# Moving one load and one conversion in a queue of weight preparations, and its last pieces to a later stage

## Chip, core and metric

One core of one Trainium2 chip runs the whole program in one launch. The metric is the device time of an execution in microseconds (us), the median of several runs. Lower is better.

## The reference

Chunked attention with a little memory, then two multilayer perceptrons (MLPs) on its 3072 rows of 512 values. Both MLPs go 512 to 2048 to 512. All weights arrive as float64.

```python
a = softmax(scale * q_c @ k_full.T)      # 32 rows, 64 or fewer keys
x = a @ v_full                           # -> 3072 x 512
h = x @ moe_w_in;   g = h - np.tanh(h);  x = g @ moe_w_out
h = x @ moe2_w_in
g = np.where(h >= 1, h, np.where(h <= -1, 0.0, (h + 1)**2 / 4))
return g @ moe2_w_out
```

## The kernel before

Products keep nearly full float32 precision by splitting each operand into a rounded high part and the remainder, `hi` and `lo`, and adding three matmuls (hi with hi, hi with lo, lo with hi).

**Steps.** MLP 1 and most of the attention run in 96 steps, 6 blocks of 512 rows by 16 slices of the hidden width. In the loop over `i`, step `i` does this in the program's order: ScalarE (ACT) rounds slice `i+2` of the input weights to its high part (`whi`, line 172), VectorE (DVE) subtracts to get the low part (`wlo`, line 179); ACT and DVE split an older gated slice (`ghi` line 214, `glo` line 215); SyncE (SP) issues DMAs; TensorE (PE) does the 12 matmuls of `hidden(i+1)` (line 559); ACT takes its tanh (line 572) and DVE subtracts it (line 573); then the events named `behind` run, and PE does the 12 matmuls of `output(i-16)` (line 597). The tanh of step `i` writes the buffer that the `glo` of the same step still reads, so ACT's tanh comes after DVE's `glo`. Each engine works its instructions off in program order, and SP does so with its DMAs, waits included. From step 30 on, every fourth step also has a group of attention; its exponentials (line 428) are on ACT, its transposes (lines 446 and 480) on PE. The last 2 blocks of MLP 1's output product, and all of MLP 2, use a scheme of seven products (Strassen's) that needs prepared weights.

**The three stages after that.** In stage G the output product of the last two blocks is made in 7 passes of 8 products, `("G", -1, k)`, k from 0 to 55 (`last_product`, line 886; six matmuls each). Then MLP 2 runs in three parts of products named `("P", sb, q, i)` and `("G", sb, k)`.

**The queue.** Weight preparation for MLP 2 is cut into pieces in the list `todo`. Each step calls `work(c)` last among its `behind` events: `c` is added to a credit, and pieces are taken, their cost deducted, as long as the credit is above 0. There are 16 slice pairs, n = 0 to 15; "n.0" and "n.1" below are the two slices of pair n. For a slice,

- `load` is one 512 KB DMA from SP (line 125) into `stage0` or `stage1`. It must wait until the buffer's last reader is done;
- `act` is two instructions on ACT (lines 137 and 140);
- `mag` is two on DVE (lines 146, 147) and `sign` two more on DVE (lines 155, 160), the last readers of the stage buffer.

A pair then has sums of quarters on DVE (line 210), rounded high parts on ACT (`prep_hi`, line 237), low parts on DVE (`prep_lo`, line 243), and stores from SP (`prep_store`, lines 314, 316). The pieces of the special weights for stage G (`own`) are put at the head of the queue at steps 48, 52, 56, 60, 66, 70, 74 and 78. In stage G and in MLP 2, `work` is called after each product.

Of the kernel before, what the change touches and what calls it, by code (L numbers as in the profile page):

```python
# [77 lines left out]
def tile_memory_attention_two_mlps(  # L78
# [40 lines left out]
    def load_weights(phase, which, fc, tag=None):  # L119
        src = ((w1_in, w1_out), (w2_in, w2_out))[phase][which]  # L120
        if tag is None:
            tag = f"stage{loaded[0] % STAGES}"
            loaded[0] += 1
        stage = wide.tile([128, 512, 2], I32, tag=tag, name=f"stage{phase}{which}_{fc}")
        nc.sync.dma_start(out=stage, in_=src[fc])
        stage_t[phase, which, fc] = stage
# [3 lines left out]
    def round_act(phase, which, fc, part=None, tag=None):  # L130
        stage = stage_t[phase, which, fc]
        low, high = stage[:, :, 0], stage[:, :, 1]
        if part != 1:
            t = slot(tag or (f"raw1_{fc % 3}" if which else f"raw0_{fc}"), f"raw{phase}{which}_{fc}")
            raw_t[phase, which, fc] = t

            nc.scalar.activation(out=t, in_=high.bitcast(F32), func=AF.Abs)
        if part != 0:

            nc.scalar.activation(out=low, in_=low.bitcast(U32), func=AF.Copy, scale=2.0 ** -29)  # L140

    def round_mag(phase, which, fc):
        t = raw_t[phase, which, fc]
        mag = t.bitcast(I32)

        nc.vector.tensor_scalar(out=t, in0=t, scalar1=F64_LOW, scalar2=F64_HIGH, op0=ALU.max, op1=ALU.min)
        nc.vector.tensor_scalar(
            out=mag, in0=mag, scalar1=3, scalar2=0x3FFFFFF8,
            op0=ALU.logical_shift_left, op1=ALU.bitwise_and,
        )  # L150

    def round_sign(phase, which, fc):
        stage = stage_t.pop((phase, which, fc))
        bits = raw_t[phase, which, fc].bitcast(I32)
        nc.vector.scalar_tensor_tensor(
            out=bits, in0=stage[:, :, 1], scalar=-0x40000000, in1=bits, op0=ALU.bitwise_and, op1=ALU.bitwise_or
        )

        eng = nc.vector if phase else nc.gpsimd
        eng.tensor_tensor(out=bits, in0=bits, in1=stage[:, :, 0], op=ALU.add)  # L160
# [92 lines left out]
    def prep_items():  # L253
        def load(n, i):
            if n < len(PAIRS):
                w, q = PAIRS[n]
                load_weights(1, w, q + i * HALF, f"stage{i}")

        def act(n, i):
            w, q = PAIRS[n]  # L260
            round_act(1, w, q + i * HALF, tag=f"prep{i}")

        def mag(n, i):
            round_mag(1, PAIRS[n][0], PAIRS[n][1] + i * HALF)

        def sign(n, i):
            round_sign(1, PAIRS[n][0], PAIRS[n][1] + i * HALF)

        load(0, 0)
        load(0, 1)  # L270
        late = [[], []]
        for n, p in enumerate(PAIRS):
            todo.extend([
                (0.0, [(act, n, 0)] + late[0]),
                (0.9, [(act, n, 1), (mag, n, 0)] + late[1]),
                (1.2, [(sign, n, 0)]),
                (0.9, [(load, n + 1, 0), (mag, n, 1)]),
                (1.2, [(sign, n, 1)]),
                (1.4, [(prep_hi, *p, 0), (prep_sums, *p)]),
                (0.6, [(load, n + 1, 1), (prep_hi, *p, 3), (prep_lo, *p, 0)]),  # L280
                (0.4, [(prep_hi, *p, 1), (prep_lo, *p, 3)]),
                (0.6, [(prep_store, *p, 0), (prep_hi, *p, 2), (prep_lo, *p, 1)]),
                (0.6, [(prep_store, *p, 3), (prep_lo, *p, 2)]),
            ])
            late = [[(prep_store, *p, 1)], [(prep_store, *p, 2)]]
        todo.extend((0.6, x) for x in late)
# [11 lines left out]
    def work(c):  # L298
        if not todo:
            return  # L300
        credit[0] += c
        while todo and credit[0] > 0:
            cost, calls = todo.pop(0)
            credit[0] -= cost
            for f, *args in calls:
                f(*args)
        if not todo:
            spare.extend(f"prep{i}" for i in range(9))
# [560 lines left out]
    def last_product(e):  # L869
        _, sb, k = e  # L870
        i, q = PASSES[k // HALF], k % HALF
        a = i in (1, 6, 7, 4)
        if q == 0 and i in (1, 2, 5):
            bank[a] = [ps_g[0].tile([128, 512], F32, tag=f"g{c}{1 - a}", name=f"acc{i}_{sb}_{c}") for c in range(2)]
        rests()
        prepare(sb, k)
        hi_g, lo_g = gsplit.pop((sb, k))
        tag, t = w_t.pop(e)
        hi, lo = t[:, :256], t[:, 256:]
        first, last = i in (1, 2, 5) and q == 0, q == HALF - 1  # L880
        products = [(j, c) for j in range(3) for c in range(2)]
        if last:
            products.sort(key=lambda p: p[1])
        for j, c in products:
            w, g = ((hi, hi_g), (lo, hi_g), (hi, lo_g))[j]
            nc.tensor.matmul(  # L886
                bank[a][c], w[:, c * 128:(c + 1) * 128], g,
                start=first and j == 0, stop=last and j == 2, skip_group_check=True,
            )
        load_w(tag)  # L890
        flush()
        if k in SUMS_AT[sb < 0]:
            g_sums(sb, *SUMS_AT[sb < 0][k])
        for j in range(1, GSETS):
            prepare(sb, k + j)
        if last:
            done(sb, i, bank[a])
        nxt = sb + 1
        if nxt < NSB:
            for f, *args in x_at[sb < 0].get(k, ()):  # L900
                f(nxt, *args)
# [66 lines left out]
    for w in range(2):  # L968
        for fc in range(FC):
            p = fc - EARLY + w * (FC + 2)  # L970
# [6 lines left out]
    for q, o in OWN_AT.items():  # L977
        at_step(rounds, o, own, q, o - FC)
    at_step(behind, PREP_FROM - 3, prep_items)
    for i in range(PREP_FROM, NS):  # L980
        at_step(behind, i + 0.9, work, (CREDIT if i < PLAIN + 12 else (3.2,) * 4 if i < LAST else (0.85,) * 4)[i % 4])
# [110 lines left out]
    for e in plan:  # L1092
        if e[0] == "P":
            product(e)
        else:
            last_product(e)
        if e[0] == "G" and e[1:] == (-1, NG2 - 1):
            spare.extend(f"y{i}" for i in range(KC))
        if e[0] == "G" and e[1] < 0:
            work(0.5 if 12 <= e[2] < 20 else 0.25 if e[2] >= 29 else 0.0)  # L1100
        elif e[0] == "P":
            work(0.1)
    assert not todo
# [49 lines left out]
```

## Time and profile before

| | |
|---|---|
| median of 3 runs | 1108.26 us (1106.98 to 1109.68) |
| profiled execution, its own time | 1105.85 us |
| span of its trace, first to last instruction | 1104.1 us |
| granted TensorE clock, mean | 0.994 |
| busy: PE, weight load, DVE, ACT, GpSimd | 96%, 78%, 76%, 61%, 4% |
| DMA traffic | 259.37 MB, 235 GB/s on average |

Steps 30 to 79 lie at about 190 to 520 us of the span, steps 80 to 95 at 520 to 563 us, stage G at 564 to 640 us, MLP 2 behind that. The span is 1.75 us shorter than the execution's own time. The mean clock is a share of TensorE's full 2.4 GHz; its other level, 1.2 GHz, shows as 0.5.

### The profile page before, as it was taken

The numbers are of one execution on the slowest core, as the hardware profiler recorded it, in microseconds if no ns is written. First come the engines' busy times: TensorE is split into PE (matmuls) and PEld (weight loads), VectorE is DVE, ScalarE is ACT, GpSimd is POOL, SyncE is SP. The second block draws the span as 40 slices with busy tenths as digits, with TensorE's granted clock in tenths as the row PEclk, the third lists the DMA queues.
The fourth block names the chain that finished last, engine by engine and source line by source line (L and its number), as shares of the span: only waits on it lengthen the run. The fifth ranks groups of instructions, "written<-read, shape, count | busy, mean of one in ns | idle before, by whom it ended". The sixth has DMA issues, their size and how long they took to land.

```text
span 1104.1 us, 21244 instructions
## 1 busy us (share of the span) xinstructions
PE 1065.4 (96%) x7607; PEld 861.9 (78%) x7607; DVE 842.2 (76%) x1490; ACT 669.1 (61%) x1353; POOL 42.5 (4%) x38
## 2 busy tenths in 40 slices
PE   7899999999999997999999999999999999999998
PEld 3677888877787776887787888887888888888887
DVE  5699977787787886888999946688557697467854
ACT  3566766656565554565565757767377766477553
POOL 1132221000000000000000000000000000000000
PEclk9999999999999999999999999999999999999999
DMA  9997887799899898768749786677776787766674
GB/s 219 251 258 209 265 232 223 218 294 304 234 295 297 266 289 269 221 213 262 230 136 332 246 270 193 194 250 222 240 205 193 205 278 213 231 195 194 200 206 148
DMA packets 211945, 259.37 MB, mean 235 GB/s; under 512 B 65408, under 2 KB 128896, under 8 KB 211840
## 3 DMA queue, kind: packets, MB, share of 16 engines
q1 hardware_dynamic: 211840, 258.01, 78.1%
q8 instruction: 61, 1.00, 0.4%
q14 instruction: 44, 0.36, 0.1%
HBM read 199.23 MB, written 58.72 MB: 234 GB/s over the span
## 4 chain that ended last, share of the span: by engine, by line
PE 73%; DVE 10%; ACT 6%; DMA 6%; SPq 2%; issue 2%; ACTq 0%; DVEq 0%
PE acc L886 19%; PE h L559 16%; PE qa L798 12%; PE acc L597 7%; PE qc L798 6%; PE qb L798 3%; DMA stage<-w_in 2%; PE acc_-1_0_7237 L886 2%; PE acc_-1_1_7238 L886 2%; DVE glo L215 2%; ACT e L428 1%; ACT g L572 1%; DVE wlo L179 1%; DVE prepl L243 1%; PE a L460 1%
## 5 line engine op out<-in xcount | busy, mean ns | idle before, releaser
L886 PE MATMUL acc<-ghi,inG 128*128 128x512 f32 x672 | 183.2, 390 | 0.0
L572 ACT ACTIVATE g<-h 128x512 f32<-128x512 f32 x96 | 57.5, 599 | 162.8 <-DVE glo L215 97.1
L886 PEld LDWEIGHTS acc<-ghi,inG 128*128 128x128 f32 x672 | 126.2, 188 | 26.1
L215 DVE TENSOR_TENSOR glo<-g,ghi 128x512 fp32r<-128x512 f32 x174 | 117.9, 686 | 31.8 <-ACT ghi L214 31.1
L798 PE MATMUL qa<-xc,inP 128*128 128x512 f32 x576 | 139.3, 389 | 0.0
L214 ACT ACTIVATE ghi<-g 128x512 fp32r<-128x512 f32 x174 | 108.2, 631 | 46.5 <-PE acc L886 24.5
L798 PEld LDWEIGHTS qa<-xc,inP 128*128 128x128 f32 x576 | 108.2, 188 | 22.4
L559 PE MATMUL h<-xh,whi 128*128 128x512 f32 (+2 forms) x392 | 108.3, 399 | 12.0 <-ACT whi L172 8.9
L559 PE MATMUL h<-xl,whi 128*128 128x512 f32 (+2 forms) x392 | 106.7, 395 | 1.4 <-issue 1.3
L886 PE MATMUL acc<-glo,inG 128*128 128x512 f32 x336 | 107.4, 391 | 0.3 <-DVE glo L215 0.2
L559 PE MATMUL h<-xh,wlo 128*128 128x512 f32 (+2 forms) x392 | 105.7, 392 | 0.3
L179 DVE TENSOR_TENSOR wlo<-raw,whi 128x512 fp32r<-128x512 f32 x112 | 80.6, 720 | 26.8 <-ACT whi L172 26.8
L573 DVE TENSOR_TENSOR g<-h,g 128x512 f32<-128x512 f32 x96 | 66.0, 688 | 40.8 <-ACT g L572 40.5
L559 PEld LDWEIGHTS h<-xh,whi 128*128 128x128 f32 x392 | 72.2, 191 | 30.0 <-ACT whi L172 11.0
L736 ACT ACTIVATE t<-g,half 128x512 f32<-128x512 f32 x72 | 52.2, 725 | 62.2 <-DVE g L732 62.2
L559 PEld LDWEIGHTS h<-xl,whi 128*128 128x128 f32 x392 | 74.5, 192 | 18.3 <-issue 1.6
L559 PEld LDWEIGHTS h<-xh,wlo 128*128 128x128 f32 x392 | 73.9, 191 | 17.1 <-DVE wlo L179 2.0
L597 PE MATMUL acc<-ghi,whi 128*128 128x512 f32 x256 | 74.6, 406 | 1.4 <-ACT y L606 1.4
L172 ACT ACTIVATE whi<-raw 128x512 fp32r<-128x512 f32 x112 | 71.0, 634 | 7.5 <-POOL raw L160 7.4
L886 PEld LDWEIGHTS acc<-glo,inG 128*128 128x128 f32 x336 | 63.0, 188 | 14.7 <-DVE glo L215 1.8
L798 PE MATMUL qc<-xc,inP 128*128 128x512 f32 x288 | 73.1, 389 | 0.0
L597 PE MATMUL acc<-ghi,wlo 128*128 128x512 f32 x256 | 70.7, 391 | 0.0
(716 smaller groups left out, 1827.8 us busy)
## 6 DMA issues: line engine op xcount, KB each, us to landing
inP<-part SPq DMA_DIRECT2D x168, 256.0 KB, 2.9
inG<-part SPq DMA_DIRECT2D x168, 256.0 KB, 3.0
stage<-w_in SPq DMA_DIRECT2D x32, 512.0 KB, 5.6
stage<-w_out SPq DMA_DIRECT2D x32, 512.0 KB, 4.5
part<-preph SPq DMA_DIRECT2D x64, 256.0 KB, 4.5
whi<-w1o SPq DMA_DIRECT2D x48, 256.0 KB, 4.8
wlo<-w1o SPq DMA_DIRECT2D x48, 256.0 KB, 5.0
part<-prepl SPq DMA_DIRECT2D x48, 256.0 KB, 4.2
```

Of the source, the lines that this page charges most:

```text
L172: nc.scalar.activation(out=hi, in_=r, func=AF.Copy)
L179: nc.vector.tensor_tensor(out=lo, in0=r, in1=hi.bitcast(F32), op=ALU.subtract)
L214: nc.scalar.activation(out=hi, in_=src, func=AF.Copy)
L215: nc.vector.tensor_tensor(out=lo, in0=src, in1=hi.bitcast(F32), op=ALU.subtract)
L243: nc.vector.tensor_tensor(out=b, in0=src, in1=a.bitcast(F32), op=ALU.subtract)
L559: nc.tensor.matmul(hp, w[:, kc * 128:(kc + 1) * 128], x[:, kc, n0:n1], start=j == 0 and kc == 0, stop=j == 2 and kc == KC - 1,)
L572: nc.scalar.activation(out=g, in_=hp, func=AF.Tanh)
L573: nc.vector.tensor_tensor(out=g, in0=hp, in1=g, op=ALU.subtract)
L597: nc.tensor.matmul(acc_t[dm], w[:, dm * 128:(dm + 1) * 128], g, start=first and j == 0, stop=last and j == 2,)
L736: nc.scalar.activation(out=t, in_=h, func=AF.Relu, scale=0.5, bias=half)
L798: nc.tensor.matmul(o, w[:, k * 128:(k + 1) * 128], z[k], start=i in (1, 2, 5) and j == 0 and k == 0, stop=j == 2 and k == 1, skip_group_ch ...
L886: nc.tensor.matmul(bank[a][c], w[:, c * 128:(c + 1) * 128], g, start=first and j == 0, stop=last and j == 2, skip_group_check=True,)
```

## The change

Within each pair the cost of each piece, and so the order in time of the whole queue, stays. The conversion `act` of the second slice goes from the second piece to the third. The load of the second slice of the next pair goes from the seventh piece to the sixth. In stage G `work` is called with 0.4 in place of 0.5 for k from 12 to 19, and with 0.25 from k = 36 in place of k = 29. What is then left in the queue is taken by the calls with 0.1 after the first products of MLP 2, which were there before and found the queue empty.

```diff
             todo.extend([
                 (0.0, [(act, n, 0)] + late[0]),
-                (0.9, [(act, n, 1), (mag, n, 0)] + late[1]),
-                (1.2, [(sign, n, 0)]),
+                (0.9, [(mag, n, 0)] + late[1]),
+                (1.2, [(act, n, 1), (sign, n, 0)]),
                 (0.9, [(load, n + 1, 0), (mag, n, 1)]),
                 (1.2, [(sign, n, 1)]),
-                (1.4, [(prep_hi, *p, 0), (prep_sums, *p)]),
-                (0.6, [(load, n + 1, 1), (prep_hi, *p, 3), (prep_lo, *p, 0)]),
+                (1.4, [(load, n + 1, 1), (prep_hi, *p, 0), (prep_sums, *p)]),
+                (0.6, [(prep_hi, *p, 3), (prep_lo, *p, 0)]),
                 (0.4, [(prep_hi, *p, 1), (prep_lo, *p, 3)]),
...
         if e[0] == "G" and e[1] < 0:
-            work(0.5 if 12 <= e[2] < 20 else 0.25 if e[2] >= 29 else 0.0)
+            work(0.4 if 12 <= e[2] < 20 else 0.25 if e[2] >= 36 else 0.0)
         elif e[0] == "P":
             work(0.1)
```

Adding up the credits by hand gives the steps at which the moved calls run:

| call | before | after |
|---|---|---|
| act of 2.1, 4.1, 6.1, 7.1 | 35, 41, 47, 53 | 36, 42, 49, 54 |
| act of 10.1, 11.1, 13.1, 14.1 | 65, 71, 79, 88 | 67, 72, 80, 89 |
| act of 0.1, 1.1, 3.1, 5.1, 8.1, 9.1, 12.1 | 30, 33, 39, 45, 58, 63, 76 | the same steps |
| load of 1.1, 2.1, 3.1, 4.1, 5.1, 6.1 | 32, 35, 38, 41, 44, 47 | 31, 34, 37, 40, 43, 46 |
| load of 8.1, 9.1, 10.1, 14.1, 15.1 | 57, 61, 65, 85, 94 | 55, 59, 64, 84, 93 |
| load of 7.1, 11.1, 12.1, 13.1 | 51, 69, 73, 77 | same step, one piece sooner |
| pair 15: act .0, act .1, mag .1, sign .1 | G 14, 14, 18, 30 | G 15, 17, 36, 40 |
| pair 15: sums, last store | G 34, G 51 | G 45, product ("P", 0, 1, 4) |

## Rows read from the trace of the kernel before

**Rows 1.** Windows: busy us of PE, weight load, DVE, ACT, GpSimd; clock, DMA share, GB/s.
```profile
225.00:523.00 298.00, 280.77 (x2504) 226.51 (x2502) 236.85 (x463) 169.65 (x439) 0.00 (x0) 0.98 0.87 266
...
564.00:640.00 76.00, 74.16 (x325) 60.49 (x325) 72.50 (x126) 48.55 (x86) 0.00 (x0) 1.00 0.82 269
640.00:1104.00 464.00, 460.14 (x2026) 379.87 (x2024) 318.21 (x498) 291.16 (x482) 0.00 (x0) 1.00 0.71 212
```
**Rows 2.** Waits of PE, 225 to 523: us in total, times, longest.
```profile
PE h L559 <- ACT whi L172: 6.8, 3, 4.3
```
**Rows 3.** Waits of DVE, 225 to 523: first two and last of eight.
```profile
DVE g L573 <- ACT g L572: 26.1, 36, 0.7
DVE wlo L179 <- ACT whi L172: 17.0, 13, 5.3
...
DVE prepl L243 <- ACT preph L237: 0.5, 1, 0.5
```
**Rows 4.** Line 572 (tanh), 225 to 515: what ended ACT's idle time before it.
```profile
  DVE glo L215: 89.0, 42
```
**Rows 5.** Timeline of ACT: start, us, instruction, in brackets idle time before and releaser.
```profile
232.99 0.68 ACT L137 ACTIVATE raw<-stage 128x512 f32<-128x512 f32 x1 [0.54 <-DMA stage<-w_in]
...
273.66 0.66 ACT L137 ACTIVATE raw<-stage 128x512 f32<-128x512 f32 x1 [1.59 <-DMA stage<-w_in]
...
435.83 0.66 ACT L137 ACTIVATE raw<-stage 128x512 f32<-128x512 f32 x1 [4.07 <-DMA stage<-w_out]
...
436.94 0.61 ACT L172 ACTIVATE whi<-raw 128x512 fp32r<-128x512 f32 x1
```
**Rows 6.** Timeline of DVE: the `wlo` behind a moved conversion.
```profile
234.75 0.69 DVE L179 TENSOR_TENSOR wlo<-raw,whi 128x512 fp32r<-128x512 f32 x1 [1.25 <-ACT whi L172]
...
275.41 0.69 DVE L179 TENSOR_TENSOR wlo<-raw,whi 128x512 fp32r<-128x512 f32 x1 [2.86 <-ACT whi L172]
...
354.64 0.69 DVE L179 TENSOR_TENSOR wlo<-raw,whi 128x512 fp32r<-128x512 f32 x1 [0.69 <-ACT whi L172]
...
437.58 0.69 DVE L179 TENSOR_TENSOR wlo<-raw,whi 128x512 fp32r<-128x512 f32 x1 [5.35 <-ACT whi L172]
```
**Rows 7.** Chain that ended last, in order of time: start, us, what.
```profile
275.43 4.62 PE h L559 x12
...
437.60 5.49 PE h L559 x12
...
446.11 2.72 PE h L559 x12
```
**Rows 8.** Timeline of PE: hidden products that waited for `whi`.
```profile
275.43 1.36 PE L559 MATMUL h<-xh,whi 128*128 128x512 f32 x4 [1.92 <-ACT whi L172]
...
437.60 2.08 PE L559 MATMUL h<-xh,whi 128*128 128x512 f32 x4 [4.28 <-ACT whi L172]
...
523.15 1.20 PE L559 MATMUL h<-xh,whi 128*128 128x512 f32 x4 [1.77 <-ACT whi L172]
```
**Rows 9.** Windows, behind the wait of 4.28 us.
```profile
437.60:441.00 3.40, 3.40 (x8) 2.72 (x9) 3.40 (x6) 2.05 (x4) 0.00 (x0) 0.50 0.99 333
```
**Rows 10.** Timeline of SP: DMA issues, start and us on the queue.
```profile
259.06 0.93 SPq L197 DMA_DIRECT2D whi<-w1o  x1
...
422.53 4.01 SPq L358 DMA_DIRECT2D k<-qkv_t  x4
...
430.71 0.59 SPq L125 DMA_DIRECT2D stage<-w_out  x1
```
**Rows 11.** Timeline of DVE: end of `sign` of slice 3.1.
```profile
263.07 0.69 DVE L160 CUSTOM_DVE_ANT_0 raw<-stage,raw 128x1024 uint16<-128x1024 uint16 x1
```
**Rows 12.** Timelines of ACT and DVE behind step 49.
```profile
325.93 0.67 ACT L172 ACTIVATE whi<-raw 128x512 fp32r<-128x512 f32 x1
...
328.14 0.69 DVE L179 TENSOR_TENSOR wlo<-raw,whi 128x512 fp32r<-128x512 f32 x1
```
**Rows 13.** Waits of PE, 523 to 640: the second of four.
```profile
PE acc_-1_0_7619 L886 <- DMA inG_-1_26_7513<-part: 1.0, 1, 1.0
```

## Prediction

> **What bounds the kernel now.** The page comes first: PE is busy 96% of the span, so there are about 40 us to be had at most, and the question is where they lie and who holds PE up. The windows answer the first part [rows 1]. MLP 2, from 640 us on, has PE busy 460.1 of 464 us: nothing to gain there, only to lose. Stage G has 1.8 us of idle PE in 76 us. The steps in which the queue runs, 225 to 523 us, have 17.2 us of idle PE, and every reason that the waits of PE give there is an instruction of ACT; the largest is `whi`, 6.8 us in three waits [rows 2].
>
> So I read who holds ACT and DVE. The waits of DVE list eight reasons in that stretch, all of them instructions of ACT; from the first to the last none names PE or a DMA [rows 3]. ACT's tanh in turn is ended by DVE's `glo` 42 times [rows 4]. The reader is to see a ring: ACT rounds `whi`, DVE makes `wlo` and `glo`, ACT does the tanh, DVE subtracts it, works its share of the queue, and the next `whi` follows. DVE never waits for PE in these 298 us. The ring therefore sets the pace of the steps, although DVE is busy only 79% of the stretch; PE runs behind it with two steps of buffers, and idles when it has caught up. What the change is worth by 523 us is what it takes off the ring.
>
> Three times the ring stands because ACT has reached the second `act` of a pair before its slice has landed: 0.54, 1.59 and 4.07 us [rows 5], for slices 2.1, 4.1 and 10.1. The worst shows why. The load of 10.1 was called in step 65, behind that step's nine transfers for the attention; SP is still issuing them at 422.5 and gets to the load at 430.7 [rows 10], 5 us before ACT goes on [rows 5]. ACT's `whi` stands behind that `act`, DVE's `wlo` behind `whi`, and PE's next product as well: 4.28 us of idle PE [rows 8], then the lower clock, 0.50 or 1.2 GHz [rows 9].
>
> **The change part by part.**
>
> *The conversion two pieces later.* For 2.1, 4.1, 7.1 and 10.1 the `act` leaves a step in which DVE waited for the `whi` queued behind it, and those four waits are 1.25, 2.86, 0.69 and 5.35 us [rows 6]. They go to nothing where `whi` is then ready before DVE is free. Without the second `act`, `whi` starts where that began to wait or to run: at 232.4, 272.1 and 431.8 (start less wait [rows 5]). Add 0.6 for `whi` itself [rows 5]: 233.0, 272.7 and 432.4. DVE comes free at 233.5, 272.6 and 432.2 (start less wait [rows 6]). So 1.25 goes entirely, of 2.86 some 2.8 and of 5.35 some 5.2. For 7.1 the wait of 0.69 is shorter than the `act`, 1.1 us of ACT's turn (435.83 to 436.94 [rows 5]), and goes. Sum: 1.25 + 2.8 + 5.2 + 0.7 = 10.0 us off the ring.
>
> The conversions arrive in another step, 1.1 us of ACT each. There DVE does the subtraction of the tanh and two `sign` instructions, some 0.69 each by the length of such instructions [rows 11, 12], 2.1 us in all, while ACT does `act` and then `whi`, 1.7 us: the cover is DVE's own work. It is thinnest where step 49 already has three pieces of `own`: `whi` starts at 325.9, DVE takes it at 328.1 [rows 12]; with 1.1 and 0.6 more it is ready at 327.6, 0.5 us early. I take nothing for the arrivals; the bound is 8 moved conversions of 1.1 us, 8.9 us, if no cover holds.
>
> Slices 6.1, 11.1, 13.1 and 14.1 I put at nothing. None of the waits in rows 6 stands behind them. 13.1 looks like a gain, since PE waits 1.77 us for the `whi` behind it [rows 8], but that `whi` also stands behind the two copies of the block's results, which take turns with DVE's two, and DVE reaches those when it did before.
>
> *The load one piece sooner.* The issue itself is 0.6 us of SP [rows 10]. For 10.1 it passes the nine attention transfers. Elsewhere it can be issued no sooner than the `sign` in the piece just ahead of it is done. In step 40 SP would have issued its next pair of weights at 259.1 [rows 10], but 3.1's `sign` ends only at 263.8 [rows 11]: SP now stands there 4.7 us, with a pair of MLP 1's weights, nine attention transfers and the stores of pair 3 behind it. The pairs are loaded two steps ahead of PE's use, and a step takes (520 - 190) / 50 = 6.6 us; the attention's operands are loaded longer ahead, and DVE is never seen waiting for a DMA. I take nothing; the bound is in the rivals.
>
> The Trainium skill, "DMA: Bandwidth & Descriptors", section "Anatomy of one DMA", speaks against this part: a semaphore wait is spent by the issuing sequencer before dispatch, so a load issued early holds up all that follows. The trace agrees that transfers queue behind one another on SP [rows 10]; by that rule alone the sum would be the slower rival below.
>
> *Stage G and MLP 2.* Pair 15's second `mag` and `sign`, four DVE instructions or at most 4 x 0.69 = 2.8 us, and its sums leave k = 18 to 34 for k = 36 to 45. DVE is busy 72.5 of 76 us in stage G [rows 1], and of PE's 1.8 us of idle time 1.0 is a wait for a DMA [rows 13], so at most 0.8 for DVE. That DMA stands behind the eight loads of x and the four stores of pair 14; the same transfers precede it after the change, so PE would only come to that landing sooner and wait longer. I take 0, with 0.8 to be gained. The six stores and the last four DVE instructions that now fall to MLP 2 lie in a stretch where DVE is busy 69% [rows 1]; without that cover they would cost 4 x 0.69 = 2.8 us.
>
> *What is late next.* Off the ring is not off PE. PE gets back more at 10.1 than the ring does: 4.28 and 5.49 - 2.72 = 2.77 of slow product [rows 7], 7.05 against 5.2. So it is up to 1.9 us further ahead when it reaches the wait for the copies at 521 us, and that wait grows from 1.77 to as much as 3.7 us. Waits of 1.92 and 4.28 us were followed by products at the lower clock, 4.62 and 5.49 us in place of 2.72; the wait of 1.77 was not, its first four matmuls taking 1.20 [rows 7, 8]. I take one such slow product, at the lower row: 4.62 - 2.72 = 1.9 us. From there on PE sets the pace and it counts.
>
> Sum: -10.0 + 1.9 = -8.1 us: 1105.85 becomes 1097.75 for the profiled execution. The median of the runs shown stands 2.4 us above that execution, and 1108.26 - 8.1 = 1100.2. A measurement tells about 0.2%, 2.2 us, from no change.
>
> **The rivals.**
>
> *No slow product at 521* (and stage G may gain its 0.8 besides): 1098.3, at best 1097.5. For it: PE's lead may be used up in small waits for ACT's exponentials before 521. Against: the waits of 1.92 and 4.28 us both had a slow product behind them [rows 7, 8].
>
> *PE keeps all it gets back.* Then the sum is PE's own: 6.8 us of waits for `whi` [rows 2] and 1.9 + 2.77 of slow products, 11.5, or 1096.8. For it stand the lists of PE; against it rows 3. The Trainium skill, "Perfetto Trace Analysis", section "Identifying the Most-Contended Engine", would have it so, taking the engine with the highest occupancy; by it the time would be these 1096.8.
>
> *The arrivals land on the ring.* 8.9 us come back, 1109.1, no change; with half of them 1104.6. For it: the margin of 0.5 us in step 49. Against: rows 3 and 4, by which ACT mostly waits for DVE.
>
> *Slower: SP stands in the wrong place.* The load is pulled in front of other steps' transfers eight times before `sign` is done, at most 4.7 us each. If the stores of `prep_hi` parts land that much later, the next pair's `prep_hi`, which overwrites the same buffers on ACT, waits for them; half of 8 x 4.7 is 18.8 us, 1100.2 + 18.8 = 1119. It decides from the point where such waits put more than the 8.1 us of the sum on the ring. For it: the DMA engines are busy 87% of the stretch [rows 1]. Against: none of DVE's reasons names a DMA now [rows 3].
>
> *It doesn't do what it says:* the loads, pulled forward, land no sooner because the queue of transfers, not the place in it, is slow; then `act` still waits less by being two pieces later, and half the sum stays, 1104.
>
> **How the numbers follow.** Forecast 0.45 (its own range 1099 to 1102), no slow product 0.2, PE keeps it all 0.1, arrivals 0.1 (half of them still a gain), slower 0.07, not as it says 0.08. Likeliest: 1100.2. With the two faster rivals at the low end and the halved sums at the high end, 1096.5 to 1105 holds 8 in 10. Faster by over 0.2%: 0.45 + 0.2 + 0.1 and half of the 0.18 of the partial cases, 0.83; within: 0.1; slower: 0.07.
>
> **What would show it.** Right: no DMA of `stage` in ACT's waits; DVE's total wait for `whi` between 225 and 523 us down from 17.0 to about 7; no product of 5.49 us near 430; the load of 10.1 issued before its step's attention transfers; a longer wait than 1.77 before the product at (now) 513 us, with the clock at 0.5 behind it. Wrong: DVE or ACT waiting for a DMA, `wlo` waiting for `whi` in steps 37, 43, 50 or 55, new idle PE from 640 us on.

## The result and the profile after

The changed kernel takes 1097.91 us, the median of 4 runs (1097.07 to 1099.58). The kernel before, run 4 times beside it, takes 1107.77. The ratio is 0.991 (95% interval 0.9892 to 0.9928): 9.9 us faster. The forecast was 1100.2, within 1096.5 to 1105. The profiled execution takes 1097.07 us with a span of 1095.3 us; before it was 1105.85 and 1104.1.

The windows of the changed kernel, in the columns of [rows 1], for the queue's stretch, stage G and MLP 2 (the last two begin 8 us sooner now):

```profile
225.00:523.00 298.00, 284.49 (x2545) 229.61 (x2544) 244.58 (x477) 173.90 (x446) 0.00 (x0) 1.00 0.89 275
556.00:632.00 76.00, 74.67 (x327) 60.88 (x326) 72.02 (x124) 48.16 (x86) 0.00 (x0) 1.00 0.80 257
632.00:1095.00 463.00, 459.28 (x2022) 378.82 (x2020) 318.94 (x499) 291.69 (x483) 0.00 (x0) 1.00 0.73 215
```

The same 298 us hold more work of PE (2545 matmuls for 2504), and PE still idles 13.5 us in them. MLP 2 idles 3.7 us, as before (3.9). So the time was won in the queue's stretch. What DVE waits for there, from 225 to 516 us, in the columns of [rows 3] (first two and last of eight reasons):

```profile
DVE g L573 <- ACT g L572: 26.7, 36, 1.0
DVE wlo L179 <- ACT whi L172: 8.1, 10, 1.2
...
DVE prepl L243 <- ACT preph L237: 0.5, 1, 0.5
```

The window of [rows 3] ends just ahead of the last of these waits, 1.18 us at 523.13, which the window here takes in. With it, from 226 to 524 us, the kernel before has:

```profile
DVE wlo L179 <- ACT whi L172: 18.2, 14, 5.3
```

So the wait of `wlo` for `whi` fell from 18.2 to 8.1 us, its longest from 5.3 to 1.2, and still no reason names PE or a DMA. The fall is the four waits of [rows 6], 10.15 us; the ten that are left stood there before. ACT now finds each moved slice landed. Its timeline, in the columns of [rows 5]: the second slices 2.1, 4.1 and 10.1, and the `whi` behind the last of them.

```profile
236.44 0.66 ACT L137 ACTIVATE raw<-stage 128x512 f32<-128x512 f32 x1
...
275.29 0.68 ACT L137 ACTIVATE raw<-stage 128x512 f32<-128x512 f32 x1
...
437.84 0.66 ACT L137 ACTIVATE raw<-stage 128x512 f32<-128x512 f32 x1
...
438.99 0.62 ACT L172 ACTIVATE whi<-raw 128x512 fp32r<-128x512 f32 x1
```

No bracket stands behind them: the waits of 0.54, 1.59 and 4.07 us are gone. DVE's timeline over the arrival of 10.1 shows the cover that the forecast counted on:

```profile
439.26 0.69 DVE L155 SCALAR_TENSOR_TENSOR raw<-stage,raw 128x512 int32<-128x512 int32 x1
439.99 0.69 DVE L160 CUSTOM_DVE_ANT_0 raw<-stage,raw 128x1024 uint16<-128x1024 uint16 x1
440.59 0.69 DVE L179 TENSOR_TENSOR wlo<-raw,whi 128x512 fp32r<-128x512 f32 x1
```

`whi` ends at 439.61, and DVE, busy with the two `sign` instructions, takes it at 440.59 without a wait.

SP's issues, in the columns of [rows 10], at step 40 and for slice 10.1:

```profile
258.33 0.42 SPq L197 DMA_DIRECT2D wlo<-w1o  x1
263.63 0.33 SPq L125 DMA_DIRECT2D stage<-w_in  x1
...
265.38 0.39 SPq L352 DMA_DIRECT2D q<-qkv_t  x1
...
417.86 0.44 SPq L125 DMA_DIRECT2D stage<-w_out  x1
...
419.99 6.17 SPq L358 DMA_DIRECT2D k<-qkv_t  x4
```

The load of 10.1 now goes out ahead of its step's attention transfers, at 417.9 in place of 430.7. At step 40 SP stands from 258.75 (258.33 + 0.42) to 263.63, 4.9 us, with nine attention transfers behind it, and none of the waits of DVE, ACT or PE shows that.

A ruler for all runs below: the time from the first matmul of hidden product 37, as the queue's pieces set in, to that of product 82, behind which they end. Before it runs from 226.49 to 523.15, 296.66 us; after from 227.64 to 514.76, 287.12. That is -9.54. The first part of the profiled execution was 1.15 us longer (a spell of 6.8 us at clock 0.50 began at 30.1, ahead of everything that was changed), and what follows product 82 was 0.4 us shorter: 1.15 - 9.54 - 0.41 = -8.80, the difference of the spans. That start differs from run to run by up to 4 us, which the ruler leaves out. DVE's waits are compared over the same stretch in every kernel below, the wait just ahead of product 82 included.

### The profile page after: what moved, and what is told of

Read it like the earlier page. It is cut to its first block, busy times and chain, and to the rows that moved or that the text cites. A ratio compares the mean times of both kernels' runs of the same rounds, so it can differ in the third digit from the quotient of the medians.

```text
span 1095.3 us, 21230 instructions
## 1 busy us (share of the span) xinstructions
PE 1060.5 (97%) x7601; PEld 858.1 (78%) x7607; DVE 842.7 (77%) x1490; ACT 669.5 (61%) x1353; POOL 42.6 (4%) x38
## 4 chain that ended last, share of the span: by engine, by line
PE 67%; DVE 18%; ACT 7%; DMA 3%; issue 2%; SPq 2%; DVEq 0%; ACTq 0%
PE acc L886 20%; PE qa L798 12%; PE h L559 11%; PE qc L798 6%; PE acc L597 5%; PE qb L798 3%; DVE wlo L179 2%; DVE glo L215 2%; ACT g L572 2%; PE acc_-1_0_7237 L886 2%; PE acc_-1_1_7238 L886 2%; DVE g L573 2%; ACT e L428 2%; DVE sums L210 2%; DVE raw L155 1%
## 5 line engine op out<-in xcount | busy, mean ns | idle before, releaser
L559 PE MATMUL h<-xl,whi 128*128 128x512 f32 (+2 forms) x392 | 104.2, 388 | 0.1
```

The source lines that it names most:

```text
L559: nc.tensor.matmul(hp, w[:, kc * 128:(kc + 1) * 128], x[:, kc, n0:n1], start=j == 0 and kc == 0, stop=j == 2 and kc == KC - 1,)
```

## Experiments

The theory under test: a ring of ACT and DVE sets the pace here, and the conversion moved later is what took the waits off it. Rivals: PE, with the highest share of busy time, sets the pace; or the sooner load made the gain.

**One part alone.** Three kernels, each with one part of the diff shown above.

```diff
# the load alone
-                (1.4, [(prep_hi, *p, 0), (prep_sums, *p)]),
-                (0.6, [(load, n + 1, 1), (prep_hi, *p, 3), (prep_lo, *p, 0)]),
+                (1.4, [(load, n + 1, 1), (prep_hi, *p, 0), (prep_sums, *p)]),
+                (0.6, [(prep_hi, *p, 3), (prep_lo, *p, 0)]),
# the conversion alone
-                (0.9, [(act, n, 1), (mag, n, 0)] + late[1]),
-                (1.2, [(sign, n, 0)]),
+                (0.9, [(mag, n, 0)] + late[1]),
+                (1.2, [(act, n, 1), (sign, n, 0)]),
# the passes alone
-            work(0.5 if 12 <= e[2] < 20 else 0.25 if e[2] >= 29 else 0.0)
+            work(0.4 if 12 <= e[2] < 20 else 0.25 if e[2] >= 36 else 0.0)
```

The load alone:

> Only the load of the second slice is pulled one piece forward; the conversion and the late stages stay as before. Ring theory (DVE and ACT set the pace up to 523 us): 10.1 lands at about 426, so the wait of 4.07 us goes, but the conversion still takes 1.1 us of ACT in front of the next whi, ready at 433.5 against DVE free at 432.2: 5.35 becomes 1.3, 4.0 gained. 4.1 likewise: issued when the sign of 3.1 is done, 263.8, whi ready at 273.8 against 272.6, 1.6 gained. 2.1 gains nothing, since SP already stood at that sign, and 7.1 nothing. Sum 5.6: 1102. Rival, the load is what counts: the whole 9.9, 1098. Rival, the conversion's place is what counts: 0, 1108.

The conversion alone:

> Only the conversion of the second slice goes to the third piece; the load and the late stages stay as before. Ring theory: all four waits go, 10.0 us, because 10.1 has landed at 435.8 and its conversion, in step 67, is not due before 437; 1098, as the full change. Rival, the load is what counts: the waits for the DMA stay in part, 1104 or more.

The passes alone:

> Only the credits in stage G change, so that pair 15's last pieces come later and in part among MLP 2's products. My theory: 0, at best 0.8 gained, because the wait for a DMA in stage G takes up what DVE gives back; 1107 to 1108. Rival, the relief of DVE in stage G is worth something by itself: 2 us or more, 1105.5. Rival, the pieces cost PE in MLP 2: slower by 2.8 us, 1110.5.

| kernel | median, us | ratio to before (95%) | product 37 to 82, us | DVE's wait for `whi` there, us |
|---|---|---|---|---|
| before, beside the three | 1107.17 | | 296.66 | 18.2 |
| load alone | 1100.39 | 0.9937 (0.9922 to 0.9952) | 290.28 | 11.7 |
| conversion alone | 1098.14 | 0.9914 (0.9899 to 0.9929) | 286.96 | 8.0 |
| passes alone | 1107.43 | 0.9999 (0.9989 to 1.001) | 296.85 | 18.2 |
| all three, beside a before of 1107.77 | 1097.91 | 0.991 (0.9892 to 0.9928) | 287.12 | 8.1 |

The conversion alone gives all of it: the load of 10.1 still goes out only at 426.2, behind the attention transfers, lands at 431.1, and ACT comes to it at 436.9. The load alone takes 6.4 us of ring, more than half, by itself; 5.6 was expected, with nothing for slice 2.1, whose wait fell by 0.6. The two don't add up: they are two ways to take off the same waits. What the load alone leaves is seen in its timelines of ACT and DVE around slice 10.1, first ACT's:

```profile
429.73 0.71 ACT L137 ACTIVATE raw<-stage 128x512 f32<-128x512 f32 x1
430.30 0.71 ACT L140 ACTIVATE stage<-stage 128x512 int32<-128x512 uint32 x1
430.85 0.67 ACT L172 ACTIVATE whi<-raw 128x512 fp32r<-128x512 f32 x1
```

and DVE's next low part:

```profile
431.55 0.69 DVE L179 TENSOR_TENSOR wlo<-raw,whi 128x512 fp32r<-128x512 f32 x1 [1.18 <-ACT whi L172]
```

The DMA is out of it: no bracket at 429.73. But the 1.1 us of the second conversion still stand ahead of `whi`, and DVE waits 1.18 us in place of 5.35 [rows 6]. Only the later place of the conversion takes that part too. The passes alone give nothing that a measurement can tell.

**A load on one engine of the ring.** To the changed kernel one instruction on 128x256 values of a tile of its own is added in each of the steps 33 to 78, 46 in all, behind the queue's pieces: in one kernel on DVE, in another on ACT.

```diff
+    scratch = const.tile([128, 256], F32, name="scratch")
...
+    def extra():
+        nc.vector.tensor_tensor(out=scratch, in0=scratch, in1=scratch, op=ALU.subtract)
+    # the other kernel: nc.scalar.activation(out=scratch, in_=scratch, func=AF.Copy)
+    for i in range(33, 79):
+        at_step(behind, i + 0.95, extra)
```

On DVE:

> The changed kernel with one more DVE instruction of 256 columns (about 0.34 us of its turn) behind the queue's pieces in each of steps 33 to 78, on a tile of its own that nobody else reads. Ring theory: it adds 46 x 0.34 = 15.6 us, 1113.5. Rival, PE sets the pace and DVE, busy 79% there, has room: 0 to 2 us, 1098 to 1100.

On ACT:

> The changed kernel with one more ACT instruction of 256 columns (about 0.31 us of its turn) behind the queue's pieces in each of steps 33 to 78, on a tile of its own that nobody else reads. Ring theory: in most steps ACT has to wait for DVE's glo anyway and it is hidden; it counts only where DVE waits for whi or for a rounded half, some 12 of the 46 steps, 4 us: 1102. Rival, ACT is as much the pace as DVE: 46 x 0.31 = 14 us, 1112. Rival, PE sets the pace: 0, 1098.

On DVE: 1109.32 us, ratio to before 1.0016 (1.0005 to 1.0026), 11.4 above the changed kernel, and 300.59 us from product 37 to 82, 13.5 more (the profiled execution had 2.3 us less ahead of product 37). The lines of these two kernels stand two further down. The waits of DVE from 225 to 526 us, the group for `whi`:

```profile
DVE wlo L181 <- ACT whi L174: 5.7, 8, 1.2
```

and the largest group of PE's waits:

```profile
PE b L482 <- ACT e L430: 10.4, 7, 2.0
```

The wait for `whi` shrank from 8.1 to 5.7, so 2.4 of the added 15.6 us (46 times 0.34, from one such instruction to the next in DVE's timeline) fell into time in which DVE stood anyway; 15.6 - 2.4 = 13.2, about what the ruler shows. The expectation had left that out; the rival, in which DVE has room, gave 0 to 2. DVE is busy for 249.05 of 298 us there, 84%, and yet passes nearly all of the added work on. PE, which has no more to do than before, just waits longer for ACT's exponentials. On ACT the same number of instructions costs little: 1100.36 us, ratio 0.995 (0.9936 to 0.9965) beside a before of 1106.34, and 289.50 from product 37 to 82, 2.4 more. ACT has room, except where `whi` stands behind it: DVE's wait for `whi` rises from 8.1 to 10.9, and 0.6 of waits for the tanh goes. So by the ruler the DVE instructions cost 13.5 / 2.4, between five and six times as much as those of ACT. PE as the bound of this stretch is out: 46 instructions that never touch it cost 11.4 us by the medians and 13.5 by the ruler.

**What is left on the ring.** If the remaining 8.1 us of waits for `whi` are worth their length, rounding it sooner should pay again. First `whi` of the next slice was put ahead of the queue's pieces on ACT in every step from 30 on:

```diff
+    for i in range(PREP_FROM, NS - 3):
+        at_step(behind, i + 0.85, split_weights_hi, i + 3, 0)
...
-            split_weights_hi(i + 2, 0)
+            if i <= PREP_FROM:
+                split_weights_hi(i + 2, 0)
```

> The changed kernel, and from step 30 on ACT rounds the next step's weights (whi) just ahead of the queue's pieces, no longer behind them. Ring theory: DVE's ten remaining waits for whi between 220 and 516 us, 8.1 us in all in the changed kernel, go, but ghi, which stays behind the pieces, now ends some of them 0.6 us later in the place of whi; 4 to 6 us gained, 1092 to 1094. Rival, PE has become the limit: 0, 1098.

It took 1096.02 us, ratio 0.9901 (0.9885 to 0.9918), beside a before of 1106.34: by the interval no different from the change alone, and not the 4 to 6 us that were expected. It needs 286.68 us from product 37 to 82, only 0.4 less. The waits of DVE, 225 to 516 us, five of eight reasons:

```profile
DVE sums L243 <- ACT ownh L237: 4.2, 2, 2.1
DVE preph L243 <- ACT preph L237: 3.7, 2, 1.9
DVE raw L146 <- ACT raw L137: 3.5, 3, 2.8
DVE ownl L243 <- ACT ownh L237: 2.7, 3, 1.3
...
DVE glo L215 <- ACT ghi L214: 2.0, 7, 0.6
```

The group for `whi` is gone, but `ownh`, `preph` and `raw` now stand behind `whi` on ACT, and DVE waits some 0.5 us longer for each of them: 4.2 for 3.2, 3.7 for 2.7, 3.5 for 2.2, 2.7 for 1.7. With 2.0 for `ghi`, 0.5 more for `prepl` and 0.8 more for the tanh, 7.6 of the 8.1 us came back elsewhere. The wait only moved. So it was put ahead in just the nine steps where DVE still waited for it, and the changed kernel was run beside it once more:

```diff
+    ROUNDED_AHEAD = (32, 48, 53, 57, 64, 67, 71, 75, 80)
+    for i in ROUNDED_AHEAD:
+        at_step(behind, i - 1 + 0.85, split_weights_hi, i + 2, 0)
...
-            split_weights_hi(i + 2, 0)
+            if i not in ROUNDED_AHEAD:
+                split_weights_hi(i + 2, 0)
```

> The changed kernel, with the rounding of the next slice (whi) put ahead of the step's queue pieces on ACT in just the nine steps behind which DVE still waits for it (0.35 to 1.2 us each, 7.8 us in all); in the other steps the order stays, so that no low part has to wait longer for its high part. The ring theory: the waits of 1.2 leave about 0.6 each for ghi, the others go, so some 5 to 6 us leave the ring and PE still has 13.5 us of idle time to give: 1092 to 1093. Rival: what is left of the ring's waits no longer sets the end, because PE's own waits for the exponentials do: 1097 to 1098, as the changed kernel. Slower than 1099 would say that a wait moved to another instruction costs as much as it did here.

The changed kernel again:

> The changed kernel itself once more, on the same chip as the selected rounding, so that the two compare directly: 1097 to 1099 by both theories. For the clock: if a slow spell follows a wait of PE by its length alone, the waits of 1.77 us and 2.4 us in this run are followed by one or not as in the first profile of it; if not, the spells fall elsewhere.

The nine steps: 1092.05 us (1091.35 to 1097.56, 6 runs), ratio 0.9871 (0.9849 to 0.9893). The changed kernel: 1097.18 (1095.78 to 1098.6, 5 runs), ratio 0.9906 (0.9889 to 0.9923). The difference of the medians is 5.1 us; the two intervals overlap just at their edges, but the ruler says the same, 282.68 against 287.05. This is the fastest version here. Its waits of DVE, 225 to 511 us, three of nine reasons:

```profile
DVE preph L243 <- ACT preph L237: 2.7, 2, 1.4
...
DVE glo L215 <- ACT ghi L214: 2.0, 7, 0.6
...
DVE wlo L179 <- ACT whi L172: 0.7, 2, 0.3
```

and its window for the queue's stretch:

```profile
225.00:523.00 298.00, 290.13 (x2563) 235.89 (x2562) 248.62 (x484) 176.07 (x451) 0.00 (x0) 0.99 0.90 279
```

7.3 us of waits for `whi` left the list (8.0 in the run beside it, to 0.7); 2.0 came back as waits for `ghi`, 0.8 as longer waits for the tanh (27.5 for 26.7) and 0.4 for `raw` (2.6 for 2.2): 4.1 net, and 4.4 on the ruler. PE's idle time falls from 13.5 to 7.9 us.

## Why the prediction was right, and which step of it was not

**What bounds the kernel: right.** The ring set the pace. What DVE's listed waits and its added work come to is what the ruler shows, with PE's own work the same: 9.5 us less for 9.54 measured in the change, 6.5 for 6.38 with the load alone, 9.6 for 9.70 with the conversion alone, 4.1 for 4.37 with the nine steps; 2.2 more for 2.38 with the work on ACT, 13.9 for 13.5 with that on DVE.

**The conversion two pieces later: right, 10.0 forecast, 9.5 to 9.7 measured** on the ruler (9.54 and 9.61 in the two runs of the change, 9.70 with the conversion alone). The four waits of [rows 6] are gone whole, 10.15 us, and over the window that the forecast named, up to the wait at product 82, 17.0 fell to 6.9, where it said about 7. What came back, 0.56 us, stands in DVE's timeline of the changed kernel:

```profile
280.74 0.69 DVE L573 TENSOR_TENSOR g<-h,g 128x512 f32<-128x512 f32 x1 [1.00 <-ACT g L572]
...
353.55 0.69 DVE L573 TENSOR_TENSOR g<-h,g 128x512 f32<-128x512 f32 x1 [1.00 <-ACT g L572]
```

These two waits for the tanh are 1.00 us in place of 0.72. The kernel with the conversion alone has them too, that with the load alone has none over 0.7, so it is the moved conversion that brings them; what holds the tanh up there stays open. The second isn't the price of an arrival, since ACT comes to 7.1 only at 354.37, behind it. Up to product 82 no wait of DVE for `whi` is new, so the cover held: 0.28 twice against the 8.9 of the rival. Behind it PE waits 0.72 us for `wlo` at 545.55, with the conversion alone as well, where before it waited 0.34 for `whi`: 0.4 more at most.

**The load one piece sooner: nothing, beside the other part, and right so.** With it 1097.91, without it 1098.14. The fear about SP came true as an event (it stood 4.9 us at step 40, 4.7 forecast) and cost nothing. By "Anatomy of one DMA" of the page "DMA: Bandwidth & Descriptors" in the Trainium skill, whose section is on the path from GpSimd, a wait on a semaphore is spent on the issuing sequencer before dispatch. The trace shows as much of SP, since the next attention transfer goes out at 265.38 in place of about 260.6, but no wait of PE, DVE or ACT names those operands, so they had at least 4.8 us to spare. What the forecast didn't say is that this load alone would have been worth 6.4 us. The rival "it doesn't do what it says" fell too: the load of 10.1 does land sooner, and without that the gain would be whole all the same, not half.

**Stage G and MLP 2: right.** The passes alone give a ratio of 0.9999. In the whole change PE idles 1.3 us in stage G in place of 1.8, inside the 0.8 that was left open, and it does wait longer for the DMA of [rows 13], 1.2 for 1.0. Its two waits for DVE's `glo` there, 0.2 and 0.6, are gone; the conversion alone still has them.

**What is late next: wrong.** This is the failed step: the slow product at 521 us, +1.9 of the sum. The forecast gave PE a lead of 1.9 us, a longer wait for the copies at 521, and a product at the lower clock behind it. PE's timeline of the changed kernel:

```profile
301.05 1.20 PE L559 MATMUL h<-xh,whi 128*128 128x512 f32 x4 [2.38 <-ACT xh L486]
...
504.22 0.96 PE L559 MATMUL h<-xh,whi 128*128 128x512 f32 x3 [1.05 <-ACT xh L486]
...
514.76 1.20 PE L559 MATMUL h<-xh,whi 128*128 128x512 f32 x4 [1.77 <-ACT whi L172]
```

The wait is 1.77 us, to the hundredth as before, and the product behind it runs at full clock. (In the window from 514.70 to 517.70 the granted clock is 1.00.) The lead was spent ahead of it. Before, PE has no wait at all from 441 to 520 us; after, from 441 to 512:

```profile
PE h L559 <- ACT xh L486: 1.0, 1, 1.0
PE b L480 <- ACT e L428: 0.5, 2, 0.3
```

So the last wait of a stretch doesn't grow by what PE gained: at each attention group PE meets ACT's exponentials and waits there until the ring has come as far. The chain that ended last shows the same. Before, it runs on PE's products from 437.6 to 509 us almost without a break, as PE was working off the stall of 4.28 us; the last of them, and then the longest pieces of that stretch after:

```profile
506.63 2.74 PE h L559 x12
```

```profile
427.72 2.71 DMA v<-qkv_t
451.22 1.95 ACT preph L237 x5
514.76 16.64 PE h L559 x72
```

After, between 430.5 and 514.8, no product of PE stands in it: the chain lies on ACT and DVE. (Before, it goes over to PE through a gap of 0.05 us ahead of one DVE instruction at 509.42. DVE's waits name no PE there, so this part shows that PE ran without a break, not that the ring waited for it.) The rival "no slow product at 521" described this, small waits for the exponentials included, and gave 1098.3 on the median's scale; without the 1.9, the sum is that rival, and 1097.91 was measured. "PE keeps all it gets back" came to 1096.8, near in time but wrong in its reason: PE had 13.5 us of idle time left, and work added on DVE alone moved the time. By matmul time PE is the busiest engine of the stretch, by weight loads it isn't: 226.5 us of 298, and DVE 236.9 [rows 1].

A slip in the forecast's working: its chances of a faster kernel add up to 0.84, not 0.83.

## What to carry to other kernels

Find the engines that wait only for each other, and price a change by what leaves that ring's waits, not by the busiest engine's idle time: here DVE, busy 82% of the stretch, passed on nearly all that was added to it, and PE, busy 95%, passed on nothing of a product that the clock had made 1.6 us longer. Compare waits over the same stretch of work, not the same microseconds: one wait at a window's edge hid 1.2 us here. When two edits aim at one wait, run each alone before crediting both. An instruction put ahead of others in a queue makes those wait; put it ahead only in the steps where it is the one waited for, and check what now stands behind it.

## What the runs showed of the hardware

A wait of the same length was followed by the lower clock in some runs and not in others. The wait of 2.36 to 2.38 us for `xh` near 300 us had matmuls at a granted clock of 0.50 (1.2 GHz) behind it in five kernels (load alone, conversion alone, passes alone, added ACT work, nine steps) and none in both runs of the changed kernel; a wait of 2.01 us at that place was followed by it before. The wait of 1.76 to 1.77 us for `whi` was followed by it once, with the passes alone, in six profiles with that wait. There PE's timeline has:

```profile
526.04 1.65 PE L559 MATMUL h<-xh,whi 128*128 128x512 f32 x4 [1.77 <-ACT whi L172]
```

and the window behind it, in the columns of [rows 1]:

```profile
526.60:530.00 3.40, 3.40 (x9) 2.63 (x8) 2.60 (x5) 0.40 (x1) 0.00 (x0) 0.50 1.02 336
```

So the forecast's reading, that 1.92 us brings a slow product and 1.77 doesn't, can't be told from a single profile. The Trainium skill, "TensorE: Matmul & The Clock Gate", section "What's actually happening", says that the chip's look at the activity runs free of the kernel; these profiles agree as far as they go. What a slow product costs depends on where it falls. Near 300 us it cost nothing. The conversion alone has one there, and the changed kernel doesn't, in their windows:

```profile
301.90:305.20 3.30, 3.30 (x9) 2.55 (x9) 3.20 (x8) 0.27 (x1) 0.00 (x0) 0.50 1.00 311
```

```profile
301.00:304.40 3.40, 3.34 (x13) 2.46 (x14) 3.01 (x8) 2.04 (x4) 0.00 (x0) 1.00 1.02 321
```

With it, PE takes 7.47 us from this hidden product to the next (300.18 to 307.65), without it 5.90 (301.05 to 306.95). Yet the conversion alone needs 286.96 us from product 37 to 82, the changed kernel 287.12. The 1.57 us go into waits that PE has otherwise: in the changed kernel it waits 0.99 for ACT's copy just behind, with the conversion alone it doesn't.

```profile
312.24 1.33 PE L597 MATMUL acc<-ghi,whi 128*128 128x512 f32 x4 [0.99 <-ACT y L606]
```

Behind the ring's end it counts. With the added work on ACT, PE waited 2.06 us ahead of product 82:

```profile
516.77 2.08 PE L561 MATMUL h<-xh,whi 128*128 128x512 f32 x4 [2.06 <-ACT whi L174]
```

The product took 4.41 us to the next one, where the changed kernel has 2.86, and the time from product 82 to the end is 582.1 us for 580.5. With the passes alone it is 582.8, before 581.0, though a wait for a DMA in stage G was also 1 us longer there. So the price that the forecast put on a slow product at 521 us, 1.9, was near; it was the longer wait ahead of it that didn't come.
